# Whole rows for the first weight loads, two loads issued by ScalarE, and a shared last copy

## The chip, the cores and the metric

The kernel runs on one core of a Trainium2 chip. The metric is device time of one execution in microseconds (us), the median of several runs; a profile of one execution shows what each engine did: TensorE (PE, with its weight loads PEld), VectorE (DVE), ScalarE (ACT), GpSimd (POOL), and SyncE (SP), which only issues transfers. Sixteen DMA engines move the data, whichever engine issues a transfer. The DRAM side of this kernel is 36.55 MB read and 25.56 MB written.

## The reference, cut to what matters

A dynamic convolution makes a new value of each token from the seven latest tokens, with weights that are a softmax over seven taps for each of eight heads. A maxout network follows: two products with 192x1024 matrices, their larger one, and a product back to 192.

```python
w = np.exp(w - np.max(w, axis=-1, keepdims=True))       # (8, 4160, 8 heads, 7 taps)
w = w / np.sum(w, axis=-1, keepdims=True)
out = np.einsum('bshk,bskhg->bshg', w, x_unf)           # x_unf: the 7 latest rows of x
x = out.reshape(33280, 192)
h1 = x @ w1                                             # (192, 1024)
h2 = x @ w2
g = np.maximum(h1, h2)
return (g @ w_out).astype(np.float32)                   # (33280, 192)
```

## The kernel before, in words

The 33280 tokens lie as 260 columns of 128 partitions. They are worked in batches of 16 columns (a few are smaller), a batch in units of 4 or 8 columns. For a unit, ScalarE takes the exponentials of the weights (`X`, L153), VectorE sums them (`n`, L168), ScalarE takes the logarithm (`l`, L172), VectorE subtracts it (`s`, L177) and ScalarE writes the normalized weights in bf16 (`W`, L191). VectorE multiplies them with `x` (`m`, L211) and adds the seven taps. TensorE then makes the hidden products (L336), ScalarE keeps their positive part (L346), and TensorE multiplies it by `w_out` (L376, L388). The maximum is had as h1 + relu(h2 - h1), so what TensorE needs of w1 and w2 is their difference `wd` and, for the linear part, the product of w1 and w_out (`w10`).

The matrices have 192 rows. The first 128 rows of w1 and w2 are staged in the tiles `ws0E` and `ws1E` (128 partitions x 1024), the last 64 rows in `ws0T` and `ws1T` (two halves of 512 columns, one above the other: 128 partitions x 512). `load_w(h, wi)` (L563, issue at L566) brings half `h` of the first rows of matrix `wi` as 128 runs of 2048 bytes; `load_last(h, wi)` (L571, issue at L574) brings half `h` of the last rows, 64 runs of 2048 bytes, to partitions 64h to 64h+63. All are issued by SyncE.

The start of the kernel is written out by hand as a list of steps, `OPENING` (L721). Each engine takes its own steps of that list in the order in which they stand. The steps that matter here: `lg.0` and `lg.1` load the convolution weights of the first two batches (`wg_t`), `xf` the first columns of x (`xs`, two transfers), `lt.h.wi` and `lw.h.wi` call `load_last` and `load_w`, `lx` loads further columns of x (`xb`) through GpSimd, `k.n` runs n matmuls on nothing but the identity (`warm`, L674), `xa` and `xv` cast `xs` to bf16 on ScalarE and VectorE (L700), `c.i` casts a 512-column block of w1 to bf16 on ScalarE (L622; c.0 and c.1 read the two halves of ws0E, c.2 reads ws0T), `d.i` subtracts w1 from w2 on VectorE (L597; d.0 and d.1 the halves of the E tiles, d.2 the T tiles), `t.i` swaps the halves of a difference across partitions on TensorE (L606), `T.i` copies that back to `wd` on ScalarE (L614, L616), `y` sums the taps and transposes on TensorE (L281), `e` copies that out on ScalarE (`yt`, L293), `h.t` and `r.t` are the hidden products and their relu for tile t. In ScalarE's order around the weights stand: W.0.12 (two instructions of L191), c.0, W.0.8 and W.0.4 (four of L191), c.2, e.0.0, c.1, e.0.1, T.3 and T.4, X.1, r.0.

Transfers of SyncE and ScalarE take turns on eight completion semaphores: the ninth waits until the first has landed, and so on.

From the third batch on, sums are transposed by DMA (L245) and results are stored by SyncE (L450), one transfer of 768 KB for a unit of eight columns; for the units in `PARTED` (L414, 19 to 24) it is two transfers of 384 KB. The last of all results leaves by `evac` (L416): ScalarE copies two pieces of 192 columns from two PSUM banks to `o_last` in one instruction (L422), then ScalarE and SyncE each issue the store of one piece (L425).

Of the kernel before, what the change touches and what calls it, by code (L numbers as in the profile page):

```python
# [17 lines left out]
def _sub(base: bass.AP, off: int, dims):  # L18
    ap = [list(base.ap[0])] + [[int(s), int(c)] for s, c in dims]
    return dataclasses.replace(base, offset=base.offset + off, ap=ap)  # L20
# [3 lines left out]
def kernel(  # L24
# [9 lines left out]
    nc = tc.nc  # L34

    B, S, D = x.shape
    H, K = weight_gen.shape[2], weight_gen.shape[3]
    F = moe_w1.shape[1]
    P = 128
# [3 lines left out]
    HF = F // 2  # L43
# [10 lines left out]
    def dcol(c):  # L54

        return (c + ROT) % CPP
# [207 lines left out]
    def half(j):  # L264
        return slice(64 * j, 64 * j + 64)
# [83 lines left out]
    def column(c):  # L349

        for u, (b, o, n) in enumerate(UNITS):
            k = c - BATCHES[b][0] - o
            if 0 <= k < n:
                return u, k // 2, k % 2

    def place(p):

        u, i, _ = column(2 * p)
        b, o, n = UNITS[u]
        return BATCHES[b][0] + o + i, n // 2  # L360
# [50 lines left out]
            tc.add_manual_dep(go.ins, mm.ins.name, SYNC, reason="bank of the other half")  # L411
        return go

    PARTED = range(19, 25)  # L414

    def evac(p, n):  # L416

        tile_, at = op_at[p]
        o = o_t[0]
        if p == NT // 2 - 1:  # L420

            nc.scalar.copy(out=_sub(o_last, 0, [[D, 2], [1, D]]),  # L422
                           in_=_sub(tile_, at, [[512, 2], [1, D]]))
            for j, eng in enumerate((nc.scalar, nc.sync)):
                eng.dma_start(  # L425
                    out=bass.AP(tensor=out.tensor, offset=dcol(place(p)[0] + 2 * j) * D, ap=[[CPP * D, P], [1, D]]),
                    in_=o_last[:, j * D:(j + 1) * D],
                )
            return
        runs = [[q for q in range(p, p + n) if column(2 * q)[0] == u]  # L430
                for u in range(column(2 * p)[0], column(2 * (p + n - 1))[0] + 1)]
        for qs in runs:
            c, h = place(qs[0])
            copied = nc.scalar.copy(out=_sub(o, c % 24 * D, [[D, len(qs)], [h * D, 2], [1, D]]),  # L434
                           in_=_sub(tile_, at + (qs[0] - p) * D, [[D, len(qs)], [512, 2], [1, D]]))
        stores = []
        for q in range(p, p + n):
            u, i, _ = column(2 * q)
            if u == NU - 2 and UNITS[u][2] == 8 and i % 2:
                stores.append((nc.sync, place(q)[0] - 1, [4 * D, 2], [1, 2 * D]))  # L440
            elif u < NU - 1 and i == UNITS[u][2] // 2 - 1:
                w = i + 1
                for k in range(0, 2 * w, w if u in PARTED else 2 * w):
                    stores.append((nc.sync, place(q)[0] - i + k, [1, (w if u in PARTED else 2 * w) * D]))
            if u == NU - 1:
                stores.append((nc.sync, place(q)[0], [2 * D, 2], [1, D]))
        for eng, c, *ap in stores:

            def issue(eng=eng, c=c, ap=ap, o=o):
                eng.dma_start(  # L450
                    out=bass.AP(tensor=out.tensor, offset=dcol(c) * D, ap=[[CPP * D, P], *ap]),
                    in_=_sub(o, c % 24 * D, ap),
                )

            if 3 <= u < NU - 3:
                held.append(issue)
            else:
                while u > 3 and held:
                    held.pop(0)()
                issue()  # L460
        return copied
# [9 lines left out]
    for g in range(3, len(GROUPS)):  # L471
        most = 4 if g == 3 else 2 if GROUPS[g][1] == 2 or len(OUTS[-1]) == 4 else 4
        n = min(most, ready[g] - c)
# [21 lines left out]
    def hidden(g, now=(), between=lambda: None, beside=lambda: None, ahead=lambda: None,  # L495
               before=lambda: None, after=lambda: None):


        t0, n = GROUPS[g]
        rd = room(g)  # L500
        for t in range(t0, t0 + n - 1):
            hid_tile(t)
        if now:
            out_room(now, "a" if n == 1 and "a" in ps else None)
            last = out_first(now)
        for t in range(t0, t0 + n - 1):
            relu(rd, t, 1)
        go = relay(last) if now else None
        hid_tile(t0 + n - 1)
        before()  # L510
        if len(now) > 2:
            beside()
        relu(rd, t0 + n - 1, 1)
        ahead()
        if now:
            out_second(now, go)
            evac(now[0] // 2, len(now) // 2)
        between()
        after()
        if len(now) <= 2:  # L520
            beside()

    def rest_of_results(c):

        parts = [p for p in (c[:4], c[4:-2], c[-2:]) if p]
        assert max(map(len, parts)) <= 4
        go = []
        for i, now in enumerate(parts):
            out_room(now, ("r", "a", "c")[i])
            go.append(relay(out_first(now)))  # L530
            if i:
                out_second(parts[i - 1], go[i - 1])
                evac(parts[i - 1][0] // 2, len(parts[i - 1]) // 2)
        out_second(parts[-1], go[-1])
        evac(parts[-1][0] // 2, len(parts[-1]) // 2)
# [10 lines left out]
    o_last = consts.tile([P, 2 * D], FP32, name="o_last")  # L546
# [5 lines left out]
    ws = {(kind, wi): stage.tile([P, w], FP32, name=f"ws{wi}{kind}") for kind, w in (("E", F), ("T", HF)) for wi in range(2)}  # L552
# [10 lines left out]
    def load_w(h, wi):  # L563

        wsrc = (moe_w1, moe_w2)[wi]
        return nc.sync.dma_start(  # L566
            out=ws["E", wi][:, h * HF:(h + 1) * HF],
            in_=bass.AP(tensor=wsrc.tensor, offset=h * HF, ap=[[F, P], [1, HF]]),
        )

    def load_last(h, wi):  # L571

        wsrc = (moe_w1, moe_w2)[wi]
        return nc.sync.dma_start(  # L574
            out=ws["T", wi][half(h), :],
            in_=bass.AP(tensor=wsrc.tensor, offset=P * F + h * HF, ap=[[F, 64], [1, HF]]),
        )
# [124 lines left out]
    def results_buffer(_):  # L702
# [5 lines left out]
    DO = {  # L708
        "Z": results_buffer,
        "xf": lambda c0, n: load_x_first(c0, n), "lw": load_w, "lt": load_last, "lo": load_wo,  # L710
        "lg": lambda b, i=0, of=1: load_wg(b, nc.sync if b < 2 else nc.gpsimd, i, of), "lx": load_x, "lh": load_halo,
        "xv": lambda c0, n: cast_x("v", c0, n), "xa": lambda c0, n: cast_x("a", c0, n),
# [6 lines left out]
    }  # L719

    OPENING = """  # L721
        lg.0 xf.-6.6 xf.0.4 lt.1.0 lt.0.0 k.2 lw.0.1 k.19 lw.0.0 lt.1.1 lw.1.0 lt.0.1 X.0.0.2 k.1 n.0.0.2
        X.0.1.2 lw.1.1 k.1 k.2 n.0.1.2 l.0.0.2 s.0.0.2 xa.-6.4 l.0.1.2 W.0.0.0 lx.0.4.4@l.0.0.2 lg.1 xv.-2.6
        W.0.0.1 s.0.1.2 W.0.12 c.0 lx.0.12.4@W.0.12 W.0.8 m.0.0.0 m.0.0.1 W.0.4 y.0.0 y.0.1 c.2 e.0.0 c.1
        e.0.1 d.0 d.2 t.0 k.3 t.2 T.3 d.1 T.4 h.0 h.1 t.1 X.1 r.0 lx.0.8.4 T.1 lo.0 r.1 m.0.4 n.1 v.0 h.2
        lx.1.0.8 V.1 y.1 r.2 l.1 h.3 e.1 m.0.8 lg.2@l.1 s.1 V.0 m.0.12 r.3 h.4 W.1.0 m.1.0 y.2 h.5 r.4 p.0
# [98 lines left out]
```

## Time and profile before

| what | value |
|---|---|
| median of 3 runs | 405.54 us (405.38 to 405.75) |
| the profiled execution's own time | 405.37 us |
| its span in the profile | 403.6 us |
| TensorE busy | 394.8 us, 98% of the span |
| VectorE busy | 369.1 us, 91% |
| ScalarE busy | 360.9 us, 89% |
| chain that ended last | TensorE 92%, ScalarE 5%, DMA 1%, SyncE's queue 1% |
| bytes moved by DMA | 63.16 MB, mean 157 GB/s |

The profile shows one execution. Times in the views are counted from the start of the span. A row of the timeline gives the start, the length, the engine, the line, the operation with the tile written and the tile read, the number of instructions, and in brackets the idle time before it and what ended that. The chain of waits is followed back from the last instruction: at each step it goes to what released that step, or to the instruction before it on the same engine. A row of a table by stretches of time gives the stretch and, for each engine, busy time and number of instructions, then the granted TensorE clock, the mean busy share of the 16 DMA engines and the rate in GB/s. For a transfer the profile gives its issue and the time from issue to landing.

### The profile page before, as it was taken

What the parts mean: (1) busy time and instruction counts of PE and PEld (TensorE: products, weight loads), DVE (VectorE), ACT (ScalarE), POOL (GpSimd) and SP (SyncE); (2) the same over time, 40 slices, a digit from 0 to 9 for tenths busy, and PEclk for the clock granted to TensorE, in tenths of its full rate; (3) what the DMA queues carried; (4) which work ended last, traced back from release to release, by engine and by line L of the source; (5) the groups of instructions that cost most, each with busy time, mean ns of one, the idle gap of its engine ahead of it and who ended that gap; (6) DMA issues with size and microseconds to landing.
All of it is one profiled execution on the core that took longest, in us unless ns stands there. A gap on an engine that the chain in (4) does not pass through costs nothing.

```text
span 403.6 us, 16321 instructions
## 1 busy us (share of the span) xinstructions
PE 394.8 (98%) x7499; PEld 321.3 (80%) x7499; DVE 369.1 (91%) x211; ACT 360.9 (89%) x466; POOL 72.3 (18%) x96
## 2 busy tenths in 40 slices
PE   7799999999999999999999999999999999999996
PEld 3589999777778777778777778877777877787996
DVE  5999999999999999999999999999999999998200
ACT  5999899999999989999899999989999899888872
POOL 3111031211122210222220122122012121200000
PEclk9999999999999999999999999999999999999999
DMA  8956468767768646864766667777457847558304
GB/s 262 222 140 151 120 124 167 183 164 133 190 110 222 182 79 129 240 187 80 217 187 107 141 192 193 99 215 198 81 115 228 178 80 200 141 106 193 104 31 169
DMA packets 60883, 63.16 MB, mean 157 GB/s; under 512 B 47641, under 2 KB 48665, under 8 KB 60816
## 3 DMA queue, kind: packets, MB, share of 16 engines
q1 hardware_dynamic: 52816, 40.15, 36.4%
q0 software_dynamic: 7856, 21.89, 27.4%
q8 instruction: 58, 0.95, 1.0%
q10 hardware_dynamic: 144, 0.10, 0.1%
q14 instruction: 9, 0.07, 0.1%
HBM read 36.55 MB, written 25.56 MB: 154 GB/s over the span
## 4 chain that ended last, share of the span: by engine, by line
PE 92%; ACT 5%; DMA 1%; SPq 1%; issue 0%
PE op_ps L376 42%; PE hdc L336 13%; PE hdb L336 13%; PE hda L336 13%; PE op_ps L388 8%; ACT rd_t L346 2%; DMA ws0E<-in_moe_w_dram 1%; PE hdp L336 1%; PE yps L281 1%; ACT en_t L191 1%; ACT yt L293 1%; ACT e_t L153 0%; ACT w1t L644 0%; SPq L574 0%; ACT w L622 0%
## 5 line engine op out<-in xcount | busy, mean ns | idle before, releaser
L376 PE MATMUL op_ps<-wo,rd_t 64*128 64x192 bf16 x4160 | 210.6, 243 | 0.0
L376 PEld LDWEIGHTS <-rd_t 64*128 64x128 bf16 x4160 | 181.0, 94 | 14.7
L211 DVE TENSOR_TENSOR m_t<-xb,en_t 128x10752 bf16<-128x10752 bf16 (+2 forms) x39 | 187.8, 4821 | 1.5 <-ACT en_t L191 1.4
L336 PEld LDWEIGHTS <-wd 64*128 64x128 bf16 x1824 | 96.8, 94 | 40.4 <-issue 2.5
L346 ACT ACTIVATE rd_t<-hdc 128x1024 bf16<-128x1024 f32 x82 | 84.1, 1025 | 17.8 <-PE hdc L336 16.2
L253 POOL CAST gate<-yt 128x1 f32<-128x1 bf16 x30 | 39.9, 1332 | 271.3 <-DMA yt<-y_t 271.3
L346 ACT ACTIVATE rd_t<-hda 128x1024 bf16<-128x1024 f32 x81 | 83.4, 1030 | 0.2 <-ACT o_t L434 0.2
L346 ACT ACTIVATE rd_t<-hdb 128x1024 bf16<-128x1024 f32 x81 | 83.5, 1031 | 0.0
L227 DVE TENSOR_TENSOR m_t<-m_t 128x4608 bf16<-128x4608 bf16 (+1 forms) x30 | 73.0, 2433 | 0.1
L336 PE MATMUL hdc<-yt,wd 64*128 64x512 bf16 (+1 forms) x552 | 67.9, 353 | 0.0
L434 ACT COPY o_t<-op_ps 128x384 f32<-128x384 f32 (+1 forms) x99 | 56.1, 577 | 12.4 <-PE op_ps L376 12.3
L336 PE MATMUL hdb<-yt,wd 64*128 64x512 bf16 (+1 forms) x540 | 67.1, 355 | 0.0
L336 PE MATMUL hda<-yt,wd 64*128 64x512 bf16 (+1 forms) x540 | 67.1, 355 | 0.0
L388 PE MATMUL op_ps<-w,yt 64*128 64x192 bf16 x780 | 55.5, 243 | 0.0
L388 PEld LDWEIGHTS <-yt 64*128 64x128 bf16 x780 | 39.0, 94 | 14.5 <-issue 0.3
L233 DVE TENSOR_TENSOR m_t<-m_t 128x3072 bf16<-128x3072 bf16 (+1 forms) x30 | 50.2, 1674 | 0.1
L191 ACT ACTIVATE en_t<-wg_t 128x896 bf16<-128x896 f32 (+3 forms) x48 | 35.7, 773 | 3.0 <-PE op_ps L376 2.0
L236 DVE TENSOR_TENSOR y_t<-m_t 128x1536 bf16<-128x1536 bf16 (+1 forms) x30 | 27.5, 916 | 0.6
L177 DVE TENSOR_TENSOR wg_t<-wg_t,sum_t 128x280 f32<-128x280 f32 (+6 forms) x46 | 22.2, 483 | 0.0
L168 DVE TENSOR_REDUCE sum_t<-e_t 128x64 f32<-128x448 f32 (+3 forms) x31 | 19.7, 639 | 2.3 <-ACT e_t L153 2.3
L125 POOL DMA_DIRECT2D xb<-in_x_dram x34 | 18.2, 537 | 17.3 <-ACT rd_t L346 11.0
L153 ACT ACTIVATE e_t<-wg_t 128x896 f32<-128x896 f32 (+2 forms) x18 | 15.9, 886 | 2.1 <-DMA wg_t<-in_weight_gen_dram 2.1
(40 smaller groups left out, 110.0 us busy)
## 6 DMA issues: line engine op xcount, KB each, us to landing
out_dram<-o_t SPq DMA_DIRECT2D x21, 768.0 KB, 4.3
xb<-in_x_dram POOLq DMA_DIRECT2D x30, 384.0 KB, 5.0
out_dram<-o_t SPq DMA_DIRECT2D x22, 384.0 KB, 3.7
wg_t<-in_weight_gen_dram POOLq DMA_DIRECT2D x13, 448.0 KB, 5.7
xb<-xb POOLq DMA_DIRECT2D x7, 288.0 KB, 5.1
wg_t<-in_weight_gen_dram SPq DMA_DIRECT2D x2, 448.0 KB, 5.2
xb<-in_x_dram POOLq DMA_DIRECT2D x4, 192.0 KB, 6.4
xs<-in_x_dram SPq DMA_DIRECT2D x1, 576.0 KB, 4.3
```

Source lines behind the costliest of these rows:

```text
L177: nc.vector.tensor_tensor(out=w_t, in0=w_t, in1=_sub(s_ts[b], hs.start, [[1, hs.stop - hs.start], [0, K]]), op=ALU.subtract)
L191: act = nc.scalar.activation(out=_sub(en_ts[b], (o * WGC + ((i or 0) * J + j) * N * K) * 2, [[2 * N, K], [2, N], [1, 2]]), in_=_sub(wg_ts[ ...
L211: return nc.vector.tensor_tensor(out=m_out, in0=x_in, in1=_sub(en_ts[b], at * H * 2, [[2, K * n * H], [0, G // 2], [1, 2]]), op=ALU.mult,)
L227: nc.vector.tensor_tensor(out=taps(0, 1, 3), in0=taps(0, 1, 3), in1=taps(3, 1, 3), op=ALU.add)
L233: nc.vector.tensor_tensor(out=taps(0, 2, 2), in0=taps(0, 2, 2), in1=taps(1, 5, 2), op=ALU.add)
L236: nc.vector.tensor_tensor(out=_sub(y_ts[b], o * D, [[64, 2], [P, 3 * w // 2], [1, 64]]), in0=taps(0, 1, 1), in1=taps(2, 1, 1), op=ALU.add,)
L253: nc.gpsimd.tensor_copy(out=gate, in_=yt[:, 0:1])
L336: nc.tensor.matmul(hid_out(t, f, j), lhsT=wd_at(j, s, f // 4, f % 4 * P, P), rhs=_sub(yt_ts[u][half(j), :], (s + j) % 3 * P, [[3 * P, w // ...
L346: relu_of[t0] = nc.scalar.activation(out=rd[:, k * 1024:(k + n) * 1024], in_=hd[:, at:at + n * 1024], func=AF.Relu)
L376: return nc.tensor.matmul(op_out(c), lhsT=rd[rows, k * 1024 + at:k * 1024 + at + P], rhs=wo[rows, f * D:(f + 1) * D], start=False, stop=(r ...
L388: nc.tensor.matmul(op_out(c + j), lhsT=yt_ts[u][half(j), (3 * i + (s + j) % 3) * P:(3 * i + (s + j) % 3 + 1) * P], rhs=w10[half(j), s * D: ...
L434: copied = nc.scalar.copy(out=_sub(o, c % 24 * D, [[D, len(qs)], [h * D, 2], [1, D]]), in_=_sub(tile_, at + (qs[0] - p) * D, [[D, len(qs)] ...
```

## The change

Three edits are made together.

1. The opening's transfers. The first 128 rows of w2 (`lw.2.1`) and of w1 (`lw.2.0`) each come as one transfer of 128 runs of 4096 bytes in place of two transfers of 128 runs of 2048. Of the four transfers of the last rows, the two for partitions 64 to 127 (`lt.1.0.1`, `lt.1.1.1`) are issued by ScalarE, ahead of its first exponential; the two for partitions 0 to 63 stay with SyncE. SyncE's order becomes: wg_t of batch 0, xs, xs, ws0T, ws1T, ws1E whole, ws0E whole, wg_t of batch 1. Before it was wg_t, xs, xs, ws0T, ws0T, ws1E half 0, ws0E half 0, ws1T, ws0E half 1, ws1T, ws1E half 1, wg_t. All other steps, the casts and differences of half blocks among them, keep their place on their engines.
2. The last copy. Each of the two pieces of 192 columns is copied by an engine of its own, the first by ScalarE, the second by VectorE, and each is stored by a queue of its own as before.
3. The stores of units 17 and 18 go in two transfers each (`PARTED` from 17).

```diff
-    PARTED = range(19, 25)
+    PARTED = range(17, 25)
...
-            nc.scalar.copy(out=_sub(o_last, 0, [[D, 2], [1, D]]),
-                           in_=_sub(tile_, at, [[512, 2], [1, D]]))
-            for j, eng in enumerate((nc.scalar, nc.sync)):
+            for j, (eng, copy) in enumerate(((nc.scalar, nc.scalar.copy), (nc.sync, nc.vector.tensor_copy))):
+                copy(out=o_last[:, j * D:(j + 1) * D], in_=tile_[:, at + 512 * j:at + 512 * j + D])
                 eng.dma_start(
...
     def load_w(h, wi):
         wsrc = (moe_w1, moe_w2)[wi]
+        at, w = (0, F) if h == 2 else (h * HF, HF)
         return nc.sync.dma_start(
-            out=ws["E", wi][:, h * HF:(h + 1) * HF],
-            in_=bass.AP(tensor=wsrc.tensor, offset=h * HF, ap=[[F, P], [1, HF]]),
-        )
-
-    def load_last(h, wi):
+            out=ws["E", wi][:, at:at + w],
+            in_=bass.AP(tensor=wsrc.tensor, offset=at, ap=[[F, P], [1, w]]),
+        )
+
+    def load_last(h, wi, act=0):
         wsrc = (moe_w1, moe_w2)[wi]
-        return nc.sync.dma_start(
+        return (nc.scalar if act else nc.sync).dma_start(
             out=ws["T", wi][half(h), :],
...
-        lg.0 xf.-6.6 xf.0.4 lt.1.0 lt.0.0 k.2 lw.0.1 k.19 lw.0.0 lt.1.1 lw.1.0 lt.0.1 X.0.0.2 k.1 n.0.0.2
-        X.0.1.2 lw.1.1 k.1 k.2 n.0.1.2 l.0.0.2 s.0.0.2 xa.-6.4 l.0.1.2 W.0.0.0 lx.0.4.4@l.0.0.2 lg.1 xv.-2.6
+        lg.0 lt.1.0.1 lt.1.1.1 xf.-6.6 xf.0.4 lt.0.0 lt.0.1 k.2 k.19 lw.2.1 lw.2.0 X.0.0.2 k.1 n.0.0.2
+        X.0.1.2 k.1 k.2 n.0.1.2 l.0.0.2 s.0.0.2 xa.-6.4 l.0.1.2 W.0.0.0 lx.0.4.4@l.0.0.2 lg.1 xv.-2.6
```

## The prediction

> **What bounds the kernel now.** I read the busy time by stretches first, since shares over the whole span mix stages. One profiled execution, time from the start of its span; after the stretch come busy time and count of TensorE, weight loads, VectorE, ScalarE, GpSimd, then granted clock, DMA share and GB/s.
>
> ```profile
> span 403.6 us, 16321 instructions
> ...
> 14.00:29.40 15.40, 13.89 (x425) 12.11 (x427) 15.28 (x7) 15.33 (x27) 2.03 (x4) 1.00 0.79 157
> 29.40:396.00 366.60, 366.60 (x6868) 300.76 (x6869) 344.69 (x194) 334.80 (x416) 65.37 (x81) 1.00 0.64 153
> 396.00:403.60 7.60, 4.02 (x98) 3.79 (x92) 0.00 (x0) 1.76 (x3) 0.00 (x0) 1.00 0.34 123
> ```
>
> From 29.4 to 396 TensorE has no idle time: 366.60 of 366.60. What can move is the time at which that stretch begins and what follows it. In the opening ScalarE (15.33 of 15.40) and VectorE (15.28) are both full, so the busy shares don't say which of them leads. The chain of waits for the first 40 us does:
>
> ```profile
> 3.98 5.95 DMA ws0E<-in_moe_w_dram
> 9.95 0.03 ACT w L622
> ...
> 10.48 1.29 ACT en_t L191 x4
> ...
> 13.55 0.98 ACT wd L614 x2
> ...
> 14.54 0.95 ACT e_t L153
> ...
> 28.28 1.03 ACT rd_t L346
> ...
> 29.36 0.83 PE hdp L336 x12
> ```
>
> The first half of ws0E lands at 3.98 + 5.95 = 9.93; ScalarE starts c.0 and is on the chain from there to 29.32, with nothing but issue gaps between; then TensorE takes over. So each us by which c.0 starts later should be a us at the end, unless something that ScalarE waits for comes earlier by as much, and it waits for nothing. The timeline confirms the wait, and shows the reserve ahead of it:
>
> ```profile
> 0.74 1.28 ACT L735 ACT_TABLE_LOAD   x1 [0.74 <-PEq L809]
> 4.11 1.04 ACT L153 ACTIVATE e_t<-wg_t 128x448 f32<-128x448 f32 x2 [2.09 <-DMA wg_t<-in_weight_gen_dram]
> 8.23 0.70 ACT L191 ACTIVATE en_t<-wg_t 128x224 bf16<-128x224 f32 x2 [0.92 <-DVE wg_t L177]
> 9.95 0.62 ACT L622 CAST w<-ws0E 128x512 bf16<-128x512 f32 x1 [1.02 <-DMA ws0E<-in_moe_w_dram]
> ```
>
> **The change, part by part: the loads.** The issues of SyncE, then the times to landing (median of the transfers that a row counts; in the last fence only the first transfer of xb is in the stretch):
>
> ```profile
> 1.19 0.89 SPq L558 DMA_DIRECT2D xs<-in_x_dram  x2
> 2.12 1.19 SPq L574 DMA_DIRECT2D ws0T<-in_moe_w_dram  x2
> 5.60 0.47 SPq L574 DMA_DIRECT2D ws1T<-in_moe_w_dram  x1
> 6.83 0.33 SPq L566 DMA_DIRECT2D ws1E<-in_moe_w_dram  x1
> 7.43 0.37 SPq L118 DMA_DIRECT2D wg_t<-in_weight_gen_dram  x1
> ```
>
> ```profile
> ws1E<-in_moe_w_dram SPq DMA_DIRECT2D x1, 256.0 KB, 6.2
> ws1T<-in_moe_w_dram SPq DMA_DIRECT2D x1, 128.0 KB, 6.3
> xs<-in_x_dram SPq DMA_DIRECT2D x1, 384.0 KB, 5.2
> wg_t<-in_weight_gen_dram SPq DMA_DIRECT2D x1, 448.0 KB, 7.1
> ```
>
> ```profile
> 5.94 0.71 POOL L125 DMA_DIRECT2D xb<-in_x_dram  x1 [3.64 <-ACT sum_t L172]
> ...
> xb<-in_x_dram POOLq DMA_DIRECT2D x1, 192.0 KB, 6.9
> ```
>
> The second xs (issued half-way through its pair, 1.65) lands at 6.85, the last ws1T at 11.90, the first xb at 12.84, the last weight (ws1E, half 1) at 13.03. Between 6.85 and 13.03 all eight weight transfers landed, 4 x 128 + 4 x 256 = 1536 KB (1573 kB), and that xb beside them. Only the first 768 KB, half of the weights, were needed to start c.0 (ws0T twice, ws1E, ws0E). After the change ws0E is whole and last, so c.0 waits until all 1573 kB are in. The rates decide when:
>
> ```profile
> 3.00:4.00 1.00, 1.00 (x4) 0.36 (x3) 0.00 (x0) 0.00 (x0) 0.00 (x0) 1.00 1.05 428
> 6.00:7.00 1.00, 1.00 (x7) 0.43 (x5) 0.50 (x2) 1.00 (x5) 0.65 (x1) 1.00 1.18 246
> 8.00:8.50 0.50, 0.50 (x4) 0.22 (x3) 0.50 (x2) 0.27 (x1) 0.00 (x0) 1.00 1.05 393
> ```
>
> The engines are full throughout (1.05 to 1.18), so neither fewer issues nor a second issuer adds rate; only quicker packets would. Runs of 2048 bytes to 128 partitions already reach 393 (8 to 8.5, between the landings of ws0T and ws0E), and longer runs, of wg_t and xs, 428 (3 to 4): on the 1049 kB of the E tiles whole rows can gain 2.67 less 2.45, 0.22 us at most. What is slow is the stretch in which the 64-row transfers are due (ws0T, issued behind xs: 246). So: E tiles 1049 kB at 410, between 393 and 428, is 2.56 us, T tiles 524 kB at 246 is 2.13 us, and ws0E lands at 6.85 + 4.69 = 11.54. Lower end: all 1573 kB at 410, 3.84 us, 10.69 (at 428, 10.5). Upper end: as slow as before with xb in front, 13.03; with the 0.94 us between ws1T's landing and xb's taken off, 12.1. I take 11.54, near the middle of these ends: part of xb will still come in front, and part of the T tiles may go faster since two are moved.
>
> c.0 then starts at 11.54 instead of 9.95: **+1.59 us** (ends +0.6 and +3.1). Queued behind it on ScalarE are W.0.8, W.0.4, c.2, e.0.0, c.1, e.0.1, T.3, r.0, in order; TensorE waits for T.3 and for yt, VectorE for W.0.4. VectorE's side:
>
> ```profile
> 11.05 0.69 DVE L597 TENSOR_TENSOR wd<-ws1E,ws0E 128x512 bf16<-128x512 f32 x1
> 11.93 0.69 DVE L597 TENSOR_TENSOR wd<-ws1T,ws0T 128x512 bf16<-128x512 f32 x1 [0.19 <-DMA ws1T<-in_moe_w_dram]
> 13.16 0.69 DVE L597 TENSOR_TENSOR wd<-ws1E,ws0E 128x512 bf16<-128x512 f32 x1 [0.54 <-DMA ws1E<-in_moe_w_dram]
> 13.77 2.96 DVE L211 TENSOR_TENSOR m_t<-xb,en_t 128x5376 bf16<-128x5376 bf16 x1
> ```
>
> It loses its two waits (0.19 and 0.54) and gets one for ws0E in front of d.0: three differences of 0.69 from 11.54 end at 13.6, so m.0.4 starts about where it did, and T.3 finds its products ready at 11.54 + 3.6 = 15.1 (3.6 is 13.55 less 9.95). What is late next is ScalarE alone.
>
> The two issues on ScalarE cost it at most 2 x 0.59 (ws0T's pair took SyncE 1.19). They fit in the 2.09 us in which it waits for wg_t after its table load; without that cover they would still stand ahead of a wait for ws0E that grows from 1.02 to about 2.6, so they cost nothing. The same reserve takes a later xs: if ScalarE's two T transfers go in front of xs, 262 kB at 246 is 1.06 us, d.0 starts at 12.1 at the latest, and T.3 is not touched. SyncE's issue of ws0E waits for wg_t's landing (4.11 at the latest, where ScalarE starts on it), over 2 us before xs is in and its turn comes: nothing. wg_t of batch 1 stands behind ws0E; X.1 needs it at 14.54 + 1.59 = 16.1, before it landed at 14.53 behind as many bytes: nothing. TensorE's and GpSimd's instructions stay as they are.
>
> **The last copy and the stores.**
>
> ```profile
> 400.05 0.48 ACT o_last L422
> ...
> L667 ACT CAST w<-pw 64x192 bf16<-64x192 f32 x2 | 0.6, 314 | 0.0
> ...
> 206.82 0.52 SPq L450 DMA_DIRECT2D out_dram<-o_t  x1
> 216.77 13.28 SPq L245 DMA_TRANSPOSE yt<-y_t  x2
> ```
>
> The copy of 2 x 192 columns ends the chain with 0.48. ScalarE's copy of 192 columns took 0.314, so 0.17 comes off; VectorE, idle since before 396, does the other beside it. No row shows VectorE copying 192 columns out of PSUM; its subtraction of 512 columns took 0.69, so between 0.2 and 0.5: **-0.17 us** (ends -0.25 and +0.05). The stores of units 17 and 18, by their order on SyncE the last ones up to the store at 206.82, add two issues of some 0.5 each; SyncE has 9 us free after that before the transposes at 216.77, and TensorE shows no idle there: nothing, with 0.1 either way for meeting other transfers.
>
> **The sum.** The profiled execution took 405.37, its span 403.6 and 1.77 around it. 405.37 + 1.59 - 0.17 = 406.79; it stands 0.17 below the median of the runs, so 407.0 against 405.54. From no change this kernel can be told by about 0.2%, 0.8 us.
>
> **Rivals.**
>
> *Full rate (406.1).* ws0E lands at 10.69, since moving two T transfers takes away the slow stretches, and no xb comes in front: +0.74 - 0.17 on 405.54, 406.1 (at 428 GB/s 405.9). For it: 428 and 393 are reached. Against: all four T transfers remain.
> [...]
>
> *Everything as slow as before (408.5).* Full rows bring nothing, and all of xb goes first: 13.03 is +3.08, less 0.17.
>
> *VectorE leads (404.6).* This ends on the other side. If VectorE's full 15.28 us is what paces the opening, not ScalarE's 15.33, then the waits that it loses count: -0.73 and -0.17. It decides only if ws0E is in by about 11.1, when d.0 is reached anyway, and ScalarE makes up its later c.0. Against: the chain names ScalarE without a break.
>
> *TensorE slows after a gap (408.0).* TensorE begins slowly; start, then length, of the first weight loads on the identity:
>
> ```profile
> 2.91 0.15 PEld L674 LDWEIGHTS <-around 128*128 128x128 bf16 x1 [0.28 <-issue]
> 3.33 0.15 PEld L674 LDWEIGHTS <-around 128*128 128x128 bf16 x1 [0.27 <-issue]
> ...
> 5.88 3.34 PEld L674 LDWEIGHTS <-around 128*128 128x128 bf16 x16 [0.26 <-issue]
> ```
>
> 0.42 us apart at first, 0.21 from 5.88, after 3.4 us of work. With T.3 late, TensorE idles from about 14 to 15.1. If that brought the slow pace back for 3.4 us, it would lose 1.7 us of work; its idle 1.51 of 14.0 to 29.4 (15.40 less 13.89) can hide some: I take +1.0, 408.0.
> [...]
>
> **How the numbers follow.** Forecast 0.55 (own range 406.4 to 407.8, ws0E from 11.0 to 12.4); full rate 0.19; as slow as before 0.12; VectorE leads 0.08; slow TensorE 0.06. Slower by over 0.2%: 0.55 + 0.12 + 0.06 = 0.73; within: 0.19; faster: 0.08. The range 405.6 to 408.5 leaves out VectorE leading and the edges of the two slow cases.
>
> **What would show it.** In the changed profile: c.0 on line 622 starts at 11.5 (10.7 to 13.0) after a wait of 2 us or more for ws0E; VectorE's three differences stand back to back; the first PE row of the chain that follows ScalarE's stands near 31.0 in place of 29.36; the last copy takes 0.31. Wrong would be: ws0E landing before 10.5, a ScalarE that waits for anything between c.0 and 28, or a TensorE with idle time after 31.

## The result and the profile after

| kernel | median | runs | ratio to before, 95% interval |
|---|---|---|---|
| before, measured beside it | 405.62 us | 405.38 to 405.75 | |
| after | 410.3 us | 409.62 to 411.27 | 1.0118 (1.0099 to 1.0137) |
| after, once more (after2) | 408.98 us (before there 405.69) | 408.51 to 409.59 | 1.0076 (1.0059 to 1.0093) |

The change makes the kernel slower, by 3.3 to 4.7 us where 1.5 were forecast, and the time is outside the forecast range. The profiled execution of after took 411.27 us, its span 409.5, which is 5.9 more than the 403.6 of before. The rows below are from that execution, the slowest of its four runs. The repeat, after2, gives a second profile.

Busy time by stretches (columns as in the prediction: TensorE, weight loads, VectorE, ScalarE, GpSimd, then clock, DMA share and GB/s):

```profile
span 409.5 us, 16321 instructions
...
9.00:13.00 4.00, 1.47 (x43) 0.74 (x43) 3.37 (x4) 0.75 (x3) 1.03 (x2) 1.00 1.04 320
13.00:18.00 5.00, 4.12 (x67) 1.95 (x58) 5.00 (x5) 4.09 (x11) 1.49 (x3) 0.51 1.21 208
18.00:23.00 5.00, 4.76 (x43) 2.96 (x45) 4.08 (x3) 3.71 (x6) 0.00 (x0) 0.50 0.62 104
23.00:25.00 2.00, 2.00 (x98) 1.87 (x96) 0.41 (x1) 2.00 (x4) 0.00 (x0) 0.91 0.00 0
```

The clock column has changed: before had 1.00 in every stretch, and here TensorE runs at half its clock from about 13.1 to 23.4. (The column reads 1.00 in the first microseconds of both kernels too, where the matmuls on the identity stand 0.42 us apart in place of 0.21; that slow beginning does not show in it.) The loss can be read off: 5.00 x 0.49 + 5.00 x 0.50 + 2.00 x 0.09 = 5.1 us of clock, so 10.3 us at one half.

The chain of waits of after, first 35 us:

```profile
1.66 7.88 DMA xs<-in_x_dram
...
9.63 0.76 DVE xb L700
...
12.31 1.56 DVE m_t L211
...
13.92 1.30 PE yps L281 x34
15.22 0.54 PE turned L606
15.76 1.28 PE warm L674 x3
17.04 0.44 PE turned L606
...
17.51 1.08 ACT wd L614 x2
...
34.92 0.83 PE hdp L336 x12
```

In before the chain went from the landing of ws0E to ScalarE. Here it goes from the landing of xs to VectorE's products, from there to TensorE's tap sums and swaps, and only then to ScalarE, at T.3. TensorE takes over at 34.92 in place of 29.36: +5.56.

The timeline of after, at the places that the prediction named (start, length, engine, line, in brackets the idle time before and what ended it):

```profile
0.74 1.28 ACT L735 ACT_TABLE_LOAD   x1 [0.74 <-PEq L809]
0.77 0.56 ACTq L574 DMA_DIRECT2D ws0T<-in_moe_w_dram  x1
1.36 0.61 ACTq L574 DMA_DIRECT2D ws1T<-in_moe_w_dram  x1
...
4.85 1.04 ACT L153 ACTIVATE e_t<-wg_t 128x448 f32<-128x448 f32 x2 [2.83 <-DMA wg_t<-in_weight_gen_dram]
...
9.63 0.76 DVE L700 CAST xb<-xs 128x1152 bf16<-128x1152 f32 x1 [2.50 <-DMA xs<-in_x_dram]
...
12.46 0.79 PE L281 MATMUL yps<-around,m_t 64*128 64x64 bf16 x42 [2.53 <-DVE m_t L211]
...
13.22 0.62 ACT L622 CAST w<-ws0E 128x512 bf16<-128x512 f32 x1 [1.56 <-DMA ws0E<-in_moe_w_dram]
```

The same cast and the same tap sums in before:

```profile
6.90 0.76 DVE L700 CAST xb<-xs 128x1152 bf16<-128x1152 f32 x1 [0.50 <-DMA xs<-in_x_dram]
9.72 0.79 PE L281 MATMUL yps<-around,m_t 64*128 64x64 bf16 x42
```

ScalarE's queue issues its two transfers at 0.77 and 1.36, while ScalarE itself still loads its table, and so ahead of the second transfer of xs. VectorE's cast of xs starts 2.73 later than before (6.90), the exponentials that need wg_t 0.74 later (4.11), and c.0 3.27 later (9.95). TensorE, which had work up to its tap sums in before, stands idle for 2.53 us in front of them, and half clock follows.

Transfers issued in the first 8 us of after (size, time from issue to landing), and two stretches:

```profile
xs<-in_x_dram SPq DMA_DIRECT2D x1, 384.0 KB, 7.9
...
ws0E<-in_moe_w_dram SPq DMA_DIRECT2D x1, 512.0 KB, 8.4
...
ws0T<-in_moe_w_dram ACTq DMA_DIRECT2D x1, 128.0 KB, 4.7
ws1T<-in_moe_w_dram ACTq DMA_DIRECT2D x1, 128.0 KB, 6.6
```

```profile
8.00:9.00 1.00, 1.00 (x6) 0.48 (x5) 0.00 (x0) 1.00 (x6) 0.00 (x0) 1.00 1.13 217
9.00:10.00 1.00, 0.93 (x5) 0.20 (x3) 0.36 (x1) 0.05 (x1) 0.00 (x0) 1.00 1.00 211
```

The second xs took 7.9 us to land where it took 5.2. From 8 to 10 us, while the second xs and the last 64-row transfers come in (landings from 9.5 to 10.4), the rate is 211 to 217 GB/s.

The end, from the chain of after:

```profile
404.00 1.99 PE op_ps L376 x48
406.01 0.33 ACT o_last L423
...
406.36 0.36 DVE o_last L423
```

The two copies stand one behind the other, 0.33 and then 0.36. From TensorE's last result to the end of the span it was 403.6 - 400.03 = 3.57 us and is now 409.5 - 405.99 = 3.51. All the profiles of this case together say the same: 3.49 to 3.68 in the seven with the old copy, 3.46 to 3.53 in eight with the new one, and 3.85 in the ninth (b_end).

The span of after adds up like this: +3.3 for the later c.0; +2.2 more up to TensorE's start at 34.92, in the stretch at half clock; +0.4 more between 47.5 and 52.6 us, in two blocks of tap sums that take 1.31 and 1.54 us on the chain in place of 1.22 and 1.23, for a reason that no run shows; -0.06 at the end. That is 5.9. The profile of after2, below, adds up without that term: 3.20 + 0.88 - 0.08 = 4.0, of a span of 407.6.

### The profile page after: what moved, and what is told of

It reads as the page before. It is cut to its first block, busy times and chain, and to the rows that moved or that the text cites. A ratio compares the mean times of both kernels' runs of the same rounds, so it can differ in the third digit from the quotient of the medians.

```text
span 409.5 us, 16321 instructions
## 1 busy us (share of the span) xinstructions
PE 399.1 (97%) x7499; PEld 322.2 (79%) x7499; DVE 369.5 (90%) x212; ACT 361.2 (88%) x466; POOL 69.7 (17%) x96
## 4 chain that ended last, share of the span: by engine, by line
PE 92%; ACT 3%; DMA 2%; DVE 1%; issue 0%; SPq 0%; DVEq 0%
PE op_ps L376 42%; PE hdc L336 13%; PE hda L336 13%; PE hdb L336 13%; PE op_ps L388 8%; PE hdp L336 2%; DMA xs<-in_x_dram 2%; PE yps L281 2%; ACT rd_t L346 1%; DVE m_t L211 1%; ACT en_t L191 0%; PE turned L606 0%; ACT yt L293 0%; ACT w1t L644 0%; PE warm L674 0%
## 5 line engine op out<-in xcount | busy, mean ns | idle before, releaser
L336 PEld LDWEIGHTS <-wd 64*128 64x128 bf16 x1824 | 96.6, 95 | 41.1 <-issue 1.9
L253 POOL CAST gate<-yt 128x1 f32<-128x1 bf16 x30 | 37.2, 1238 | 273.9 <-DMA yt<-y_t 273.9
L336 PE MATMUL hdc<-yt,wd 64*128 64x512 bf16 (+1 forms) x552 | 67.8, 353 | 0.0
L336 PE MATMUL hda<-yt,wd 64*128 64x512 bf16 (+1 forms) x540 | 67.0, 355 | 0.0
L336 PE MATMUL hdb<-yt,wd 64*128 64x512 bf16 (+1 forms) x540 | 67.0, 355 | 0.0
L433 ACT COPY o_t<-op_ps 128x384 f32<-128x384 f32 (+1 forms) x99 | 56.0, 576 | 12.4 <-PE op_ps L376 12.4
```

Of the source, the lines that this page charges most:

```text
L253: nc.gpsimd.tensor_copy(out=gate, in_=yt[:, 0:1])
L336: nc.tensor.matmul(hid_out(t, f, j), lhsT=wd_at(j, s, f // 4, f % 4 * P, P), rhs=_sub(yt_ts[u][half(j), :], (s + j) % 3 * P, [[3 * P, w // ...
```

## The experiments

The theory was this: the loads alone cost what c.0 is later; ScalarE's two issues make xs, and with it everything, later; and the gap that this leaves on TensorE brings half clock, which costs the rest. The rivals were that whole rows themselves are slow, that the loss lies in the half clock alone, and that the last copy or the parted stores have a part in it. In the edits `k.n` are matmuls on the identity whose result nothing uses: more or fewer of them change what TensorE does, and nothing that is computed. Where an edit is put on "after" or "before", that kernel is otherwise whole. "Handover" is the start of the row `PE hdp L336 x12` of the chain with which TensorE takes over from ScalarE (29.36 in before). The clock given with a run is TensorE's mean granted clock over the whole run; 1.7 us of lost clock make 0.996 of it.

**All four T transfers by SyncE, on after (a_sp).**

```diff
-lg.0 lt.1.0.1 lt.1.1.1 xf.-6.6 xf.0.4 lt.0.0 lt.0.1 k.2 k.19 lw.2.1 lw.2.0
+lg.0 xf.-6.6 xf.0.4 lt.1.0 lt.1.1 lt.0.0 lt.0.1 k.2 k.19 lw.2.1 lw.2.0
```

> The changed kernel with one thing undone: all four transfers of the last rows are issued by SyncE, behind xs. Theory 1 (ScalarE's two transfers went in front of xs and made VectorE late; that and the halved TensorE clock are most of the loss): the second xs lands near 6.85 instead of 9.54, the multiplications start near 8.1, TensorE has no gap of 2.5 us and keeps its clock, c.0 starts at 11.5 to 12.7, and the time is 407.0 to 408.2. Theory 2 (it is the late whole ws0E alone, whoever issues): c.0 stays near 13.2 and the time near 410.

Measured: 409.14 against 405.73, ratio 1.0074 (1.0044 to 1.0104). c.0 at 12.53 after a wait of 3.02 for ws0E, handover 32.81 (+3.45). So without ScalarE's issues xs comes almost as early as before (the cast at 7.48), and the whole ws0E still lands 1 us later than forecast: neither theory is the whole. TensorE had no long wait ahead of its tap sums, but 1.66 us ahead of its hidden products, and half clock came (busy time by stretches of a_sp):

```profile
9.00:13.00 4.00, 3.06 (x92) 1.92 (x90) 3.17 (x3) 0.97 (x3) 2.52 (x4) 1.00 1.03 336
13.00:18.00 5.00, 2.65 (x22) 1.41 (x23) 4.35 (x5) 5.00 (x13) 0.00 (x0) 0.98 1.33 218
18.00:23.00 5.00, 5.00 (x128) 3.77 (x124) 3.93 (x2) 4.26 (x7) 0.00 (x0) 0.68 0.27 50
```

It lost 0.02 x 5 + 0.32 x 5 = 1.7 us of clock, 3.4 us at one half. The runs of this kernel go in the order of their clock: 407.88 at a mean of 1.0, 408.75 to 410.13 at 0.994 to 0.996, and 411.44 at 0.990.

**Twelve more matmuls on the identity, on after (a_warm).**

```diff
-X.0.1.2 k.1 k.2 n.0.1.2
+X.0.1.2 k.1 k.2 k.12 n.0.1.2
```

> The changed kernel with 12 more matmuls on the identity ahead of the first tap sums, so that TensorE does not stand idle from 9.9 to 12.5; transfers as changed. If the halved clock costs time by itself: the clock stays at 1.0, T.3 starts at 16.8 (c.0 at 13.2 plus 3.6) instead of 17.5, no relu waits for the hidden products, and the time is 408.6 to 409.2, against a median of 410.3. If the clock is hidden beside ScalarE's work: 410.0 to 410.5 as before.

Measured: 408.48 against 405.73, 1.0062 (1.0044 to 1.0079), the clock 0.999 or 1.0 in every run. The timeline and the chain:

```profile
12.08 0.79 PE L281 MATMUL yps<-around,m_t 64*128 64x64 bf16 x42
...
16.77 1.08 ACT L614 CAST wd<-turned 128x512 bf16<-128x512 f32 x2
...
32.68 0.83 PE hdp L336 x12
```

c.0 starts where it did in after (13.28, +3.33), T.3 no longer waits, and the handover is +3.32. TensorE does more, and the kernel is faster: against the profile of after 2.24 us at the handover (34.92 less 32.68). With the same late loads and a full clock, the handover is as late as c.0 is: the rest beyond c.0 is the half clock, and c.0 alone is worth one for one.

**ScalarE's two issues alone, on before (b_act).**

```diff
-lg.0 xf.-6.6 xf.0.4 lt.1.0 lt.0.0 k.2 lw.0.1 k.19 lw.0.0 lt.1.1 lw.1.0 lt.0.1
+lg.0 lt.1.0.1 lt.1.1.1 xf.-6.6 xf.0.4 lt.0.0 k.2 lw.0.1 k.19 lw.0.0 lw.1.0 lt.0.1
```

> The kernel before with one part of the change alone: the two transfers for partitions 64 to 127 are issued by ScalarE ahead of its first exponential; half rows and all other orders as before. Theory 1: xs lands 2 to 2.7 us later, TensorE gets the gap of about 2.5 us and the half clock, time 409 to 410.5, nearly the whole loss. Theory 2: only 128 KB more stand ahead of the first half of ws0E, c.0 is 0.3 to 0.7 us later, time 405.8 to 406.4.

Measured: 408.58 against 405.73, 1.0067 (1.0043 to 1.0091). The timeline of the profiled run, 407.13 us, whose opening kept the full clock:

```profile
8.94 0.76 DVE L700 CAST xb<-xs 128x1152 bf16<-128x1152 f32 x1 [1.69 <-DMA xs<-in_x_dram]
...
15.24 1.07 ACT L614 CAST wd<-turned 128x512 bf16<-128x512 f32 x2 [0.70 <-PE turned L606]
```

The cast of xs is 2.04 later, c.0 at 10.87 waits for nothing, T.3 waits for TensorE's swaps, and the handover is 31.13 (+1.77). The step that the prediction put at nothing costs 1.1 to 1.6 us where the clock is nearly full (three runs at 0.998 took 406.83 to 407.35, against 405.73). Five runs at 0.994 to 0.996 took 408.3 to 409.1, and two at 0.987 took 410.8.

**The end alone, on before (b_end):** the last copy by two engines, and `PARTED` from 17, as in the change.

> The kernel before with the shared last copy and the stores of units 17 and 18 in two parts each; the opening is untouched. By the prediction -0.17 us, 405.4. By the changed kernel's rows, where VectorE's copy (0.36) starts only when ScalarE's (0.32) has ended: the last store is issued 0.2 us later, 405.6 to 405.9, not to be told from no change.

Measured: 406.57 against 405.73, 1.0012 (0.9989 to 1.0035): not told from no change. The two copies follow each other here too (400.97 and 401.32). The profile's opening, which the edit does not touch, had c.0 at 10.57 and its handover at 29.96, each 0.6 later than the profile of before; so much the opening varies between executions. The unchanged kernel varies likewise: five of its 31 runs here took 407.1 to 408.2 at full clock, and one 408.84 at 0.990.

**Whole rows alone, on before (b_rows).**

```diff
-lt.1.0 lt.0.0 k.2 lw.0.1 k.19 lw.0.0 lt.1.1 lw.1.0 lt.0.1
+lt.1.0 lt.0.0 k.2 lw.2.1 k.19 lw.2.0 lt.1.1 lt.0.1
 ...
-X.0.1.2 lw.1.1 k.1
+X.0.1.2 k.1
```

> The kernel before with whole rows alone: ws1E and ws0E in one transfer each, in the places of their first halves, two T transfers ahead of them and two behind; everything by SyncE. If a later ws0E moves the end one for one: ws0E lands at about 8.0 + 1049 kB at 410 GB/s = 10.6 to 11.0, c.0 is 0.7 to 1.1 us later, time 406.2 to 406.7; VectorE's differences may wait for the last ws1T until about 12. If whole rows cost nothing: 405.6.

Measured: 406.94 against 405.68, 1.0038 (1.0023 to 1.0054). ws0E lands at 11.21, c.0 starts at 11.23 (+1.28) and the handover is 30.65 (+1.29). From 8 to 10 us, with the E tiles due, the rate was 393 to 414 GB/s, where before had 393 with halves; from 10 us until ws0E landed it was 212 to 248, with other transfers beside it, and before had 240 to 248 from 9 to 11. So whole rows show neither a gain nor a loss of rate. What costs is that c.0 needs the whole of ws0E, and ws0E comes behind the whole of ws1E.

**A gap on TensorE alone, on before (b_gap):** `k.19` becomes `k.7`; the loads stay.

> The kernel before with 12 of the 25 matmuls on the identity taken out (they compute nothing that is used), so that TensorE stands idle for about 2.5 us ahead of the first tap sums; no transfer is touched. If a gap of 2.5 us halves the clock: clock 0.5 for 7 to 10 us from about 10 to 13, the matmuls of the first hidden products take twice as long, the relus of the opening wait, time 406.5 to 408. [...]

Measured: 407.49 against 405.68, 1.0062 (1.0029 to 1.0095), the runs from 406.45 to 411.37. The timeline of the profiled run, 410.72 us, and its busy time by stretches:

```profile
10.28 0.79 PE L281 MATMUL yps<-around,m_t 64*128 64x64 bf16 x42 [2.24 <-DVE m_t L211]
11.75 1.30 PE L281 MATMUL yps<-around,m_t 64*128 64x64 bf16 x42 [0.68 <-DVE m_t L211]
```

```profile
9.00:13.00 4.00, 2.04 (x85) 1.83 (x86) 3.89 (x4) 3.15 (x10) 2.52 (x4) 0.76 1.10 270
13.00:18.00 5.00, 4.33 (x38) 2.17 (x37) 4.58 (x5) 3.91 (x8) 0.00 (x0) 0.85 1.33 233
```

With a gap of 2.24 us ahead of the tap sums half clock comes (42 tap sums in 1.30 in place of 0.79), 0.24 x 4 + 0.15 x 5 = 1.7 us of clock, 3.4 us at one half. With loads that are those of before, taking work off TensorE makes the kernel slower: all eight runs have a clock of 0.987 to 0.996, and none of the 22 runs of before beside them is under 0.998. Five of the eight took 406.45 to 407.99. The profiled run's handover is 30.93 (+1.57). Not all of that is the clock, since xs came later in this execution too (the cast at 7.46): b_swap2 below, with the cast at 7.35 and a full clock, has its handover at 29.55, which leaves about 1.3 for the half clock. The rest of this run's loss stands later, in waits of TensorE between 24 and 60 us (from the view of waits: total, times, longest):

```profile
PE yps L281 <- issue: 3.4, 2, 2.2
```

TensorE stands for 3.4 us in two waits for nothing that the profile shows. Before has no such wait there. Both stand inside blocks of tap sums, as the +0.4 of after does. What makes them is open.

**ws0E's half ahead of ws1E's, on before (b_swap, b_swap2):** `lw.0.0` and `lw.0.1` change places, so that c.0's own half lands first. In b_swap X.1 also stands behind r.0; b_swap2 leaves X.1 alone.

> The kernel before with the two first half transfers exchanged (first half of ws0E ahead of that of ws1E), and ScalarE's exponential of batch 1 (X.1) put behind the first relu. If c.0 paces the opening: ws0E lands 1 us earlier, c.0 starts at 8.95 when ScalarE gets to it, and the time falls by 0.4 to 0.9 us, 404.7 to 405.2. If VectorE or TensorE set the pace: 405.5, no change.

> The kernel before with only the two first half transfers exchanged (ws0E ahead of ws1E), X.1 back in its place. c.0 starts 0.7 to 1.0 us earlier. If ScalarE's order behind c.0 paces the opening, 404.7 to 405.2; if the differences on VectorE and their swap on TensorE are as late (T.3 at 13.6 in the exchange with X.1 moved), 405.5 to 405.8.

Measured: b_swap 406.49 against 405.68, 1.0017 (1.0007 to 1.0026); b_swap2 405.58 against 405.69, 0.9994 (0.9986 to 1.0003). In b_swap2 c.0 starts 0.67 earlier, at 9.28, and the handover is at 29.55, none the earlier. The timeline says why:

```profile
13.65 1.07 ACT L614 CAST wd<-turned 128x512 bf16<-128x512 f32 x2 [0.70 <-PE turned L606]
```

T.3 now waits for TensorE, whose chain begins with xs. In before the same swap and T.3 stood so:

```profile
12.79 0.38 PE L606 MATMUL turned<-wd,around 128*128 128x512 bf16 x1
13.45 1.08 ACT L614 CAST wd<-turned 128x512 bf16<-128x512 f32 x2
```

The swap was done at 13.17, and ScalarE got to T.3 at 13.45: the path from xs over VectorE and TensorE was 0.3 us shorter than the path from ws0E over ScalarE. In b_swap2's execution xs was cast 0.45 later (7.35 in place of 6.90; it was 7.15 to 7.72 in all the other kernels in which SyncE alone issues the loads), and this path became the longer one. So before stands near a corner: by this profile an earlier ws0E can gain 0.3 us at most, and the runs show no gain; a later ws0E costs, and a later xs costs beyond that reserve. The loss of b_swap over b_swap2, 0.9 us, is the cost of the moved X.1.

**Once more, with the causes apart (after2, a_sp_warm, b_act_warm).** after2 is after unchanged; a_sp_warm is a_sp with the twelve matmuls of a_warm; b_act_warm is b_act with them.

> The changed kernel once more, on the chip and against the runs of before that the next three share. 1.0118 times before again, 409.6 to 411.3, with the clock of each run between 0.987 and 0.995 and the longer times at the lower clocks. If the clock has nothing to do with it, time and clock show no order.

> The changed kernel with both suspects taken away: all four transfers of the last rows by SyncE behind xs, and 12 more matmuls on the identity so that the clock stays. What is left is that c.0 waits for the whole of ws0E. The one run at full clock without the added matmuls took 407.9. If the three causes add up: clock 1.0, c.0 at 11.8 to 12.5, time 407.2 to 408.0 (+1.6 to +2.3). If whole rows were free: 405.8.

> The kernel before with the two transfers issued by ScalarE, and 12 more matmuls on the identity. The late xs alone, with the clock kept: 1.4 us, 407.0, where the runs without the added matmuls at a clock of 0.998 took 406.8 to 407.4 and those at 0.987 410.8. If the late xs costs the time and not the clock, 408.6 as without them.

Measured, against 405.69: after2 408.98, less slow than expected, with clocks of 0.990 to 0.996 and no clear order among its five times; a_sp_warm 408.06, 1.0061 (1.0039 to 1.0082); b_act_warm 407.73, 1.0042 (1.0026 to 1.0058). In after2 c.0 starts at 13.15 (+3.20), half clock lasts 3.4 us (18.59 to 22.00), and the handover is 33.44, +4.08: the loads of after again, with one stretch of half clock in place of three. TensorE's gap ahead of the tap sums was 1.24 here and 2.53 in after, because the slow beginning lasted longer and the matmuls on the identity ended at 10.95 in place of 9.93. In a_sp_warm, with the clock kept (in five of its six runs; 410.34 at 0.996 is the sixth), c.0 starts at 12.44 (+2.49) and the handover is 31.85 (+2.49). Its landing of ws0E, from the chain, and the stretches ahead of it:

```profile
5.27 7.15 DMA ws0E<-in_moe_w_dram
```

```profile
7.00:8.00 1.00, 1.00 (x7) 0.45 (x5) 0.85 (x2) 0.36 (x2) 0.00 (x0) 1.00 1.12 252
8.00:9.00 1.00, 1.00 (x6) 0.43 (x5) 1.00 (x2) 0.52 (x2) 0.00 (x0) 1.00 1.04 211
9.00:10.00 1.00, 1.00 (x6) 0.49 (x5) 1.00 (x2) 0.18 (x1) 0.51 (x1) 1.00 0.96 377
10.00:11.00 1.00, 1.00 (x7) 0.43 (x5) 1.00 (x1) 0.00 (x0) 1.00 (x3) 1.00 1.03 389
11.00:12.00 1.00, 1.00 (x11) 0.34 (x11) 0.39 (x1) 0.00 (x0) 1.00 (x2) 1.00 1.11 309
```

Here xs landed at 7.05 and the last T transfer at 9.35, so the T tiles took 2.30 us at 245 GB/s in all, as taken. The E tiles then took 3.07 us, to 12.42, where 2.56 was taken: the whole of the transfers ran at 357 GB/s in that time and not at 410, falling to 309 from 11 us on. From xs's landing on they moved 1.66 MB, of which the weights are 1.573, so other bytes seem to explain only a small part. xb, issued at 5.98, landed 8.0 us later, behind ws0E; it did not come in front as a whole. Why the rate falls is not shown.

b_act_warm kept its clock but is no clean answer: the twelve matmuls held up the tap sums (13.23 against 11.76 in b_act), and the handover was 31.75.

**Which matrix comes first (a_first, a_sp3, a_first3).** All are a_sp with more identity matmuls; the first and the last bring ws0E whole ahead of ws1E whole. a_first has twelve more, a_sp3 and a_first3 three.

```diff
-lt.0.0 lt.0.1 k.2 k.19 lw.2.1 lw.2.0
+lt.0.0 lt.0.1 k.2 k.19 lw.2.0 lw.2.1
```

> As the last kernel without ScalarE's issues and with the clock kept (408.06), but whole ws0E ahead of whole ws1E. If ScalarE's wait for the whole of ws0E is what is left of the loss: ws0E lands near 11.0 instead of 12.4, c.0 starts 1.4 us earlier, and the time falls by 1.0 to 1.4, to 406.7 to 407.1, where the differences of VectorE (d.0 still at 12.4) take over. If the differences pace it already: 408, no change.

> All four transfers of the last rows by SyncE, whole ws1E ahead of whole ws0E, and 3 added matmuls on the identity in place of 12 (with 12 the added matmuls themselves ran to 12.98 in the kernel with ws0E first and stood on the chain). If c.0's wait for ws0E is what is left: c.0 near 12.4, T.3 near 16.0, 407.5 to 408.2 in the runs at full clock.

> The same with whole ws0E ahead of whole ws1E. If ScalarE's wait is what is left of the loss: c.0 at 10.6, T.3 at 14.2 to 14.8 (the differences from 12.2 now pace it), 1.0 to 1.6 us below the kernel beside it, 406.2 to 407.0. If it is the late pair of E tiles as such, because d.0 needs both: no difference beside it.

Measured: a_first 407.96 against 405.59, 1.0046 (1.0029 to 1.0062), with c.0 at 10.62 but T.3 waiting for TensorE. It gave no clean answer, since the matmuls themselves stood on the chain, up to 12.98, with nothing to wait for. With three in place of twelve, beside each other on one chip (before 405.74): a_sp3 408.38, 1.0065 (1.0042 to 1.0087), and a_first3 406.25, 1.0015 (1.0003 to 1.0028). Their c.0 in the timeline and their handover in the chain, a_sp3 first, then a_first3:

```profile
12.41 0.62 ACT L622 CAST w<-ws0E 128x512 bf16<-128x512 f32 x1 [3.04 <-DMA ws0E<-in_moe_w_dram]
...
31.79 0.83 PE hdp L336 x12
```

```profile
10.63 0.62 ACT L622 CAST w<-ws0E 128x512 bf16<-128x512 f32 x1 [1.29 <-DMA ws0E<-in_moe_w_dram]
...
30.10 0.83 PE hdp L336 x12
```

The order of the two whole loads is worth 1.78 us at c.0 and 1.69 at the handover, and 2.1 us between the medians (part of that is clock: four of the six runs of a_sp3 had 0.996, all of a_first3 0.999 or 1.0). a_first3 is the best of the changed loads that was tried, and still not faster than before.

The shifts of all kernels in which one path leads, side by side:

| kernel | c.0 later by | handover later by | TensorE's clock up to the handover |
|---|---|---|---|
| a_first3 | 0.68 | 0.74 | full |
| b_rows | 1.28 | 1.29 | full |
| a_sp3 | 2.46 | 2.43 | full |
| a_sp_warm | 2.49 | 2.49 | full |
| a_warm | 3.33 | 3.32 | full |
| a_sp | 2.58 | 3.45 | half for 3.4 us |
| after2 | 3.20 | 4.08 | half for 3.4 us |
| after | 3.27 | 5.56 | half for 10.3 us |

Five rows at full clock give one for one to within 0.06. Half clock adds 0.87 and 0.88 for one stretch of 3.4 us, and 2.29 for three. The shifts are counted from one profile of before, and by b_end a shift is good to 0.6 us; the two shifts of a row come from one execution, and what they show is that they agree.

## Why the prediction was wrong

Three steps failed. The first two made c.0 3.27 us late in place of 1.59: about 0.9 is the load term, too small even with all transfers on SyncE, and about 0.8 is ScalarE's two issues, put at nothing. The third is that TensorE was taken to keep its pace, but for a chance of 0.06: half clock cost 2.3 us in the profile of after and 0.9 in that of after2.

*"Each us by which c.0 starts later should be a us at the end."* Right, as the table shows, while TensorE's clock is full. The engine that was named as the bound was the right one; that a second path, only 0.3 us shorter in the profile of before, also ends at T.3 was not seen. "VectorE leads" was weighed only as a way to gain.

*"ws0E lands at 11.54", +1.59.* The sign and the mechanism were right, the term too small. With all transfers on SyncE it landed at 12.4 to 12.5 (a_sp, a_sp_warm, a_sp3). In a_sp_warm xs was 0.2 later, the T tiles took 2.30 in place of 2.13, and the E tiles 3.07 in place of 2.56, since 357 GB/s stood where 410 had been taken from single stretches of half a microsecond and one. That is +0.9. With ScalarE's issues it landed at 13.1 to 13.3 (after, after2, a_warm): another +0.8, beyond the upper end of 13.03, which had been taken as the case of "as slow as before with xb in front".

*"The two issues on ScalarE ... cost nothing", "if ScalarE's two T transfers go in front of xs, ... 1.06 us, d.0 starts at 12.1 at the latest".* This failed. That they fit into ScalarE's wait was right and beside the point. What counts is where their bytes go: issued at 0.77 and 1.36, they are in flight together with wg_t and xs, which are needed first. The cast of xs came 2.0 (b_act) to 2.7 us later (after) than in the profile of before, 1.2 to 2.5 us later than in the ten other kernels in which SyncE alone issues the loads (7.15 to 7.72), and d.0 came at 13.78. The bound of 1.06 counted the bytes in front of xs at one rate. Why xs lost more than that is not shown; what is shown is its time from issue to landing, 7.9 against 5.2.

*"TensorE slows after a gap", chance 0.06, +1.0.* This came true and had far too small a chance. It was looked for around T.3, as an idle time of 1.1 us. In a_sp it came there (1.66 us idle ahead of the hidden products, then half clock from 17.8), in after2 too (1.18 us idle, half clock from 18.59). In after it came earlier and from a side not thought of, the late xs: TensorE stood 2.53 us before its tap sums. It costs 0.9 us at the handover for one stretch of 3.4 us (about 1.3 in b_gap) and 2.3 for three, and it makes the runs differ. The 0.06 was the author's estimate, and no run bears it out: half clock came after gaps of 1.18 us (after2), 1.66 (a_sp), 2.24 (b_gap) and 2.53 (after); no gap in these openings was longer. In a_sp and in b_gap 1.7 us of clock were lost, 3.4 us at one half; the length of the slow beginning varied (the matmuls on the identity pick up their pace at 5.9 us in before, 6.3 in after, about 8.4 in after2). What decides whether a gap brings half clock is not settled. a_sp, busy 3.06 of 4.00 us from 9 to 13 and 2.65 of 5.00 from 13 to 18, lost the full clock; a_warm, with 3.87 and 2.63, kept it. The profile of a_sp3, with 3.83 and 2.78 and the same 1.66 us idle ahead of its hidden products, kept it, while four of its six runs have the 0.996 of one stretch: the same program can go either way, so no single length of gap is the rule.

*What was to show it.* Of the four signs, VectorE's three differences do stand back to back (13.78, 14.39, 14.99) and ScalarE's last copy takes 0.33 (0.31 foreseen). c.0 at 13.22 lies beyond the 13.0 that was allowed, its wait was 1.56 and not 2, since ScalarE itself came late to it, and the handover is 34.92 in place of 31.0. A ScalarE that waits between c.0 and 28 was named as a sign that the prediction is wrong; it waits 0.69 ahead of T.3, 0.49 for the hidden products and 0.80 for the next swap.

*The other rivals.* Full rate (406.1) failed with the E tiles' rate and with 211 to 217 GB/s in the T stretch. That moving two T transfers takes away the slow stretches was an estimate that no run shows: ScalarE's two went beside wg_t and xs and not beside SyncE's two, so the two pairs were not seen side by side. "Everything as slow as before" (408.5) comes nearest in microseconds, by luck: b_rows alone cost only 1.3, and xb, which that rival had go first, landed at 14.3 in after, behind ws0E. "VectorE leads" (404.6) failed in sign.

*The last copy, -0.17.* It failed: -0.06. VectorE's copy waits for ScalarE's, so 0.48 became 0.33 + 0.36 on the chain. Counted from TensorE's last result, ScalarE's store is issued 0.16 earlier than before and SyncE's 0.23 later; which of the two made the end 0.06 sooner is not shown. Both copies read one PSUM tile and write one tile; which of the two makes the order was not tried.

*The stores of units 17 and 18, nothing.* No run contradicts it; with b_end's interval of -0.1% to +0.35% that is all that can be said.

*Open.* The +0.4 of after between 47.5 and 52.6 us, why the rate falls while the last E tile comes in, and the two waits of TensorE in b_gap with no releaser.

## What to carry to other kernels

When transfers that are merged or moved feed several paths, ask for each path which bytes now stand in front of its first consumer, and load that consumer's part first: the order of two whole loads was worth 1.7 to 2.1 us here, and longer runs brought no rate. A second queue did not only take issues off the first here: its bytes delayed what the first issued afterwards (the second xs, by 2.0 to 2.7 us against the profile of before) and what it had issued just before (wg_t, by 0.7 to 1.1). So give it only what is needed earliest. When a front end gets later, look at what the late data does to TensorE's idle time: a few cheap matmuls that keep it busy gave back 1.0 us (a_sp to a_sp_warm) to 2.2 us (after to a_warm) at the handover, but placed where they end after the data arrives they become the chain.

## What the runs showed of the hardware

Half clock came in pieces of 3.4 us, one (a_sp, after2, b_gap) or three of them (after, 10.3 us), after 2.24 (b_gap) and 2.53 us (after) of idle TensorE, and also after gaps of 1.18 (after2) and 1.66 us (a_sp) in a stretch in which it was busy 2.76 and 2.65 of 5.00 us (13 to 18); the same gap of 1.66 us was also seen without it (a_sp3). Two loads of 128 KB on a second queue, begun beside 448 KB and 960 KB on the first, made the last of those land 2.0 to 2.7 us later than in the profile of before, 1.6 to 2.2 times what their bytes take at the 211 GB/s of after from 9 to 10 us (262 kB, 1.24 us). ScalarE's queue issued transfers during a table load of 1.28 us. And 4096-byte runs had no better rate than 2048-byte runs: the best stretches of 1 us between 8 and 11 us with whole E tiles due showed 373 (a_sp3) to 421 GB/s (a_first3), and before reached 393 (8 to 8.5 us) and 403 (12 to 13 us) with halves.
